# Every step of the two feed-forward layers given one part of the side work: conversion, activation and preparing of x

## The chip, the cores and the metric

One core of one Trainium2 chip runs the whole program. The metric is the device time of one execution in microseconds (us). TensorE (PE in the profile) multiplies; VectorE (DVE), ScalarE (ACT) and GpSimd (POOL) do the elementwise work; SyncE (SP) issues nearly all transfers. Each engine takes its instructions strictly in the order in which the program lists them, so an instruction that waits holds up all that stand behind it on its engine.

## The reference

Attention with a bucket mask (two batches, 8 heads, 768 positions, 64 wide) gives x of 1536 tokens by 512. Two feed-forward layers follow, each with 2048 hidden columns; their weights are given in double precision:

```
h = np.maximum(x @ w_in, 0.0)
x = (h * h @ w_out).astype(np.float32)
h = x @ w2_in
sp = np.where(h > 20.0, h, np.log1p(np.exp(np.minimum(h, 20.0))))
return ((h * np.tanh(sp)) @ w2_out).astype(np.float32)
```

## The kernel before

The attention fills the first 223 us or so and is untouched by the change. What follows works on each layer in 8 groups of 256 hidden columns, so groups 0 to 7 are the first layer and 8 to 15 the second. The tokens form three blocks of 512 (blk 0, 1 and 2).

Each matrix value is held as two float32r parts, a high and a low one, and each product is three matmuls (high by high, high by low, low by high).

**Steps.** The list `steps` sets the order of TensorE. A group has 26 steps of six matmuls: 7 `up` steps for blocks 0 and 1 together (128x512 tiles), 4 `down` steps for block 2 of the group before, 7 `up` steps for block 2 alone (128x256 tiles), then 8 `down` steps for blocks 0 and 1. Group 0 has no group before it and so 22 steps. In group 8 the 4 `down` steps stand ahead of the first `up` steps.

**Seven products for eight.** The product x @ w_in of a group is a 2 by 2 by 2 product of blocks, done in seven products (`SEVEN` says which sums of blocks go in, `USES` where each product is added). The seven sums of weight blocks are formed by `weigh` into the tile `wi`, the seven sums of x blocks by `prepare` into tiles `x`. Each `up` step writes a PSUM tile `m` (5 buffers). Its `use` runs behind the next step's matmuls: it copies `m` into `h` on ScalarE, adds it to `h` on VectorE, or adds one `h` to another (half of these on VectorE, half on GpSimd).

**Activation.** When an `h` is complete, `activate` has ScalarE compute the activation and the high part `gh`, and VectorE the low part `gl`. The `down` steps multiply `gh`, `gl` by the weight tile `wo` into a PSUM tile `acc` (3 buffers), which VectorE adds to `tot` (ScalarE copies it in the first group of a layer).

**Conversion.** Weights come as pieces of 128 by 512 doubles, four to a group (two for `w_in`, two for `w_out`), staged through two buffers `stg`. Each piece passes four parts: `begin` (absolute value on ScalarE into a tile `cv`, then a clamp to the range of the conversion on GpSimd; in the second layer GpSimd also adds, since ScalarE's table holds Mish there), `shift`, `low` and `end` on VectorE. `end` also issues the load of the piece after next, and for a `w_out` piece splits it into `wo` on GpSimd at once.

**Order.** Before the change a counter `due` grows by 23/26 with each step, and each whole unit of it takes the next entry of a queue (`conv_rest`: 8 parts, 7 `weigh`, 8 parts). `prepare` puts its sum, ScalarE's copy and VectorE's subtraction one behind the other into the same step. `activate` for one `h` at a time stands ahead of the matmuls' consumers of the next step.

Of the kernel before, what the change touches and what calls it, by code (L numbers as in the profile page):

```python
# [9 lines left out]
F32 = mybir.dt.float32  # L10
# [7 lines left out]
P = 128  # L18
# [5 lines left out]

EARLY = 4

XB = 2

CB = 5
GB = 5  # L30
# [30 lines left out]
def lsh_attention_relu2_mish_kernel(ctx, tc, qT, kT, vP, proj, w_in, w_out, w2_in, w2_out, out):  # L61
# [77 lines left out]

# [5 lines left out]
    def end(k):  # L145
        m, _, hi = work.pop(k)
        i, nm, c = pieces[k]
        mu = m.bitcast(U32)
        nc.vector.scalar_tensor_tensor(mu, hi, 0xC0000000, mu, ALU.bitwise_and, ALU.bitwise_or)  # L149
        stage(k + 2)  # L150
        if nm == "i":
            whole.setdefault(i, []).append(m)
            return
# [8 lines left out]
    def weigh(i, n):  # L162
# [4 lines left out]
        how = SEVEN[n][0]  # L167

        def block(b):
            return chain[i] if b == "chain" else whole[i][b[0]][:, b[1] * 256:(b[1] + 1) * 256]  # L170

        x = block(how[0])
        if len(how) > 1:
# [6 lines left out]
        nc.gpsimd.tensor_tensor(lo, x, b32(hi), ALU.subtract)  # L180


    conv = [
        [(nm, lambda part=part, k=4 * i + 2 * (nm == "o") + c: part(k)) for nm in "i" for c in range(FC) for part in parts]
        + [("i", lambda i=i, n=n: weigh(i, n)) for n in range(7)]
        + [("o", lambda part=part, k=4 * i + 2 + c: part(k)) for c in range(FC) for part in parts]
        for i in range(2 * NG)
    ]
    for i in range(EARLY // 4):
        conv[i] = []  # L190

    xf = [xy.tile([P, PPB, TB], F32, tag="xy", name=f"xf{i}") for i in range(NBLK)]

# [433 lines left out]
    for j in range(N):  # L627
# [23 lines left out]
        for when, n, k in conv_at:  # L651
            if when == j:
                if n < len(parts):
                    parts[n](k)
                else:
                    weigh(0, k)
        if bits is not None:
# [36 lines left out]
    def prepare(layer, unit, n, u):  # L694
# [14 lines left out]
        how = SEVEN[n][1]  # L709
        hi, lo, x = t[:, 0, u, :], t[:, 1, u, :], block(how[0])  # L710
        if len(how) > 1:
            if how[-1] == "chain":
                if "chain" not in (how[0], how[2]):
                    xchain[u] = xsum[0].tile([P, TB], F32, tag=f"chain{u}", name="chain", bufs=1)
                s = xchain[u]
            else:
                s = xsum[0].tile([P, TB], F32, tag="sum", name="sum")
            s = s[:, 0:w]
            (nc.vector if u else nc.gpsimd).tensor_tensor(s, x, block(how[2]), how[1])
            x = s  # L720
        nc.scalar.activation(hi, x, AF.Copy)
        nc.vector.tensor_tensor(lo, x, b32(hi), ALU.subtract)

    tot = {}
    xchain = {}
    xsum = []

    xs = {}
    prepare(0, 0, 0, 0)
    broadcast(*done, rp, N)  # L730
    prepare(0, 0, 0, 1)
    unstack(waiting, N - 1)
    for f in calls.pop(N):
        f()
    unstack(N // QT - 2, N)
    unstack(N // QT - 1, N)
    for u in range(2):
        prepare(0, 0, 1, u)
    for j in sorted(calls):
        for f in calls[j]:  # L740
            f()
# [24 lines left out]
    def up(i, unit, n):  # L766
# [8 lines left out]
        def use():  # L775
# [9 lines left out]
            ready.extend((i, blk, f) for f, blk in done.get(n, ()))  # L785

        return use

# [14 lines left out]
    def down(i, blk, c):  # L803
# [12 lines left out]
        def use():  # L816
# [44 lines left out]
    for i in range(2 * NG):  # L861
# [4 lines left out]
    at_step = {k: n for n, k in enumerate(steps)}  # L866
    behind, later, due = [], [], 0.0

    conv_rest = [(i, nm, f) for i, fs in enumerate(conv) for nm, f in fs]
    for n_step, (f, *a) in enumerate(steps):  # L870
        i = a[0]

        if f is up:
            while todo and (i // NG, a[1], a[2]) in [x[:3] for x in todo]:
                prepare(*todo.pop(0))
            while conv_rest and (conv_rest[0][0] < i or conv_rest[0][:2] == (i, "i")):
                conv_rest.pop(0)[2]()
        else:
            while (*a[:2], 0) in ready or (*a[:2], 1) in ready:
                later.append(activate(*ready.pop(0)))  # L880
            while later:
                later.pop(0)()
            while conv_rest and conv_rest[0][0] <= i:
                conv_rest.pop(0)[2]()

        pick = ready.pop(0) if ready and len(kept) < GB else None
        use = f(*a)
        if f is down and a[2] == PPB - 1:
            del kept[i, a[1], 0], kept[i, a[1], 1]
        while later:  # L890
            later.pop(0)()
        for g in behind:
            g()
        behind = [use]
        if pick is not None:
            if pick[0] == NG and loaded[-1] == EXP_SET:
                load_table(MISH_SET)
            later.append(activate(*pick))
        for _ in range(2):
            if todo:  # L900
                prepare(*todo.pop(0))
        due = min(due + 23 / 26, 4.0)
        while due >= 1 and conv_rest:
            k, nm, g = conv_rest[0]
            free = (up, k - 1, 0, 0) if nm == "i" else (down, k - 2, 2, PPB - 1)
            if at_step.get(free, -1) > n_step:
                break
            g()
            conv_rest.pop(0)
            due -= 1  # L910
    for g in behind + later:
        g()
    while ready:
        activate(*ready.pop(0))()
    last(2 * NG - 1, 2)

# ---- launch: one core; the host lays the inputs out and takes the output as it comes
# [41 lines left out]
```

## Time and profile before

| | |
|---|---|
| median of 3 runs | 991.13 us (990.05 to 991.76) |
| the profiled execution, its own time | 990.95 us |
| its span in the trace | 988.9 us |
| mean granted clock of TensorE | 0.887 of full speed |

The span leaves out 2.05 us of the time. The trace names groups by the tiles and lines; a step is six matmuls. The bracket behind a row of the timeline is the engine's idle time ahead of it and what ended that.

### The profile page before, as it was taken

The page shows a single profiled execution, that of the slowest core. Times are in us where ns is not written, and L with a number is a line of the kernel's source. Part 1 is how long each engine was busy: PE and PEld are TensorE (multiplying, and loading weights), DVE is VectorE, ACT ScalarE, POOL GpSimd, SP SyncE. Part 2 cuts the span into 40 slices and gives each one's busy share as a digit, 9 for nine tenths or more (in the row PEclk, how much of TensorE's full clock was granted, in tenths as well). Part 3 has the DMA queues.
Part 4 walks back from the last instruction along what each step waited for, and adds up shares of the span by engine and source line. Part 5 has one row for each costly group of instructions (what it writes and reads, how often), then busy time and mean ns, then how long its engine had stood idle before and what let it go on. Part 6 is the DMA issues. An engine that isn't in the chain of part 4 may idle for free.

```text
span 988.9 us, 11870 instructions
## 1 busy us (share of the span) xinstructions
PE 798.9 (81%) x3940; PEld 674.0 (68%) x3940; DVE 622.4 (63%) x1051; ACT 472.8 (48%) x879; POOL 584.9 (59%) x629
## 2 busy tenths in 40 slices
PE   9999999995697966969687686397868677686868
PEld 6999999992476755857566574376656566574757
DVE  8989989883735564654646576626464636364655
ACT  7988888892655343343434434444232323222221
POOL 9757885314364675656566564476666666666630
PEclk9999999996588989889798898598979797978889
DMA  7787687611011011111211111011011111111103
GB/s 214 170 217 196 163 203 179 161 37 29 21 43 65 23 63 43 43 64 43 65 43 43 50 39 36 26 43 64 23 63 43 43 43 43 43 43 42 43 1 127
DMA packets 29108, 72.76 MB, mean 74 GB/s; under 512 B 5064, under 2 KB 10536, under 8 KB 29048
## 3 DMA queue, kind: packets, MB, share of 16 engines
q1 hardware_dynamic: 28824, 71.88, 25.6%
q8 instruction: 31, 0.51, 0.2%
q14 instruction: 29, 0.24, 0.1%
q10 hardware_dynamic: 224, 0.13, 0.0%
HBM read 46.14 MB, written 3.19 MB: 50 GB/s over the span
## 4 chain that ended last, share of the span: by engine, by line
PE 38%; POOL 27%; DVE 20%; ACT 7%; issue 6%; DMA 1%; SPq 0%; DVEq 0%; POOLq 0%; ACTq 0%
PE acc L813 10%; POOL cv L131 7%; PE m L773 7%; PE s L427 6%; PE acc L482 6%; PE pT L453 6%; DVE h L783 4%; DVE gl L801 4%; POOL wo L158 3%; POOL wi L180 3%; POOL h L781 3%; DVE tot L824 3%; POOL sum L175 3%; POOL cv L129 3%; DVE cv L149 2%
## 5 line engine op out<-in xcount | busy, mean ns | idle before, releaser
L773 PE MATMUL m<-x,wi 128*128 128x512 f32 (+1 forms) x1344 | 288.5, 374 | 74.7 <-DVE h L783 47.1
L773 PEld LDWEIGHTS m<-x,wi 128*128 128x128 f32 x1344 | 237.8, 217 | 125.3 <-issue 47.4
L813 PE MATMUL acc<-gh,wo 128*128 128x512 f32 x384 | 134.6, 419 | 60.7 <-DVE tot L824 55.3
L813 PE MATMUL acc<-wo,gh 128*128 128x512 f32 x368 | 125.2, 424 | 48.8 <-DVE tot L824 47.0
L131 POOL TENSOR_SCALAR cv<-cv 128x512 f32<-128x512 f32 x63 | 123.3, 1957 | 30.2 <-ACT cv L123 25.8
L813 PEld LDWEIGHTS acc<-gh,wo 128*128 128x128 f32 x384 | 77.2, 201 | 84.1 <-DVE tot L824 59.3
L138 DVE TENSOR_SCALAR cv<-cv 128x512 uint32<-128x512 uint32 x64 | 33.8, 528 | 158.3 <-POOL cv L131 158.3
L783 DVE TENSOR_TENSOR h<-h,m 128x512 f32<-128x512 f32 (+1 forms) x160 | 86.6, 550 | 65.5 <-POOL h L781 52.9
L824 DVE TENSOR_TENSOR tot<-tot,acc 128x512 f32<-128x512 f32 x164 | 108.9, 681 | 22.2 <-PE acc L813 21.5
L813 PEld LDWEIGHTS acc<-wo,gh 128*128 128x128 f32 x368 | 75.2, 208 | 68.0 <-DVE tot L824 49.9
L801 DVE TENSOR_TENSOR gl<-h,gh 128x512 fp32r<-128x512 f32 x96 | 74.7, 778 | 49.3 <-ACT h L796 30.9
L470 DVE TENSOR_TENSOR pl<-pT,ph 128x768 fp32r<-128x768 f32 x96 | 91.7, 956 | 17.0 <-ACT ph L466 9.6
L779 ACT ACTIVATE h<-m 128x512 f32<-128x512 f32 (+1 forms) x128 | 55.5, 487 | 98.1 <-PE m L773 98.1
L157 POOL TENSOR_SCALAR wo<-cv 128x512 fp32r<-128x512 f32 x32 | 19.9, 623 | 135.4 <-DVE cv L149 129.4
L443 ACT ACTIVATE e<-e,nm 128x768 f32<-128x768 f32 x96 | 89.8, 935 | 7.9 <-DVE e L434 7.7
L798 ACT ACTIVATE h<-h 128x512 f32<-128x512 f32 x48 | 30.0, 625 | 132.1 <-DVE h L783 93.4
L434 DVE TENSOR_SCALAR_CACHE_REDUCE e<-s 128x768 f32<-128x768 f32 x96 | 90.9, 947 | 0.9 <-PE s L427 0.8
L781 POOL TENSOR_TENSOR h<-h 128x512 f32<-128x512 f32 (+1 forms) x32 | 32.2, 1007 | 98.6 <-DVE h L783 98.6
L466 ACT ACTIVATE ph<-pT 128x768 fp32r<-128x768 f32 x96 | 77.7, 809 | 12.7 <-PE pT L455 7.0
L813 PE MATMUL acc<-gl,wo 128*128 128x512 f32 x192 | 79.5, 414 | 0.0
L453 PE MATMUL pT<-ident,e 128*128 128x128 f32 x576 | 78.8, 273 | 0.3 <-DVE e L434 0.2
L813 PE MATMUL acc<-wo,gl 128*128 128x512 f32 x184 | 76.4, 415 | 0.0
(149 smaller groups left out, 1386.3 us busy)
## 6 DMA issues: line engine op xcount, KB each, us to landing
stg<-in_w_in_dram SPq DMA_DIRECT2D x32, 512.0 KB
stg<-in_w_out_dram SPq DMA_DIRECT2D x32, 512.0 KB
KA<-kh SPq DMA_DIRECT2D x28, 192.0 KB
v_r<-in_vP_dram SPq DMA_DIRECT2D x8, 384.0 KB
rb<-rd SPq DMA_DIRECT2D x32, 96.0 KB
out_dram<-tot SPq DMA_DIRECT2D x11, 256.0 KB
q_r<-in_qT_dram SPq DMA_DIRECT2D x7, 384.0 KB
k_r<-in_kT_dram SPq DMA_DIRECT2D x7, 384.0 KB
```

The lines of the kernel that those rows point to most:

```text
L131: nc.gpsimd.tensor_scalar(m, m, F64_LOW, F64_HIGH, ALU.max, ALU.min)
L434: nc.vector.tensor_scalar(e.rearrange("p (h s) -> p h s", s=H2), x, MASKED, None, ALU.min, ALU.min, accum_out=nm)
L443: nc.scalar.activation(e, e, AF.Exp, bias=nm, scale=-1.0, accum_out=ssums[p, half][:, c:c + 1])
L453: nc.tensor.transpose(ps[:, c * P:(c + 1) * P], e[:, c * P:(c + 1) * P], ident)
L466: nc.scalar.activation(ph, v, AF.Copy)
L470: nc.vector.tensor_tensor(pl, v, b32(ph), ALU.subtract)
L773: nc.tensor.matmul(m, WI[i][:, n, a, fs], x[:, b, u, :], start=u == k == 0, stop=u == 1 and k == 2)
L781: (nc.gpsimd if f else nc.vector).tensor_tensor(h, h, h_of(i, unit, *how), ALU.add)
L783: nc.vector.tensor_tensor(h, h, m, how)
L801: return lambda: nc.vector.tensor_tensor(gl, h, b32(gh), ALU.subtract)
L813: nc.tensor.matmul(acc, x, y, start=f == k == 0, stop=f == FC - 1 and k == 2)
L824: nc.vector.tensor_tensor(t, t, acc, ALU.add)
```

## The change

Every part of the side work gets a step of its own, from a fixed table of offsets (`conversion`), and GpSimd keeps only the splitting of weights, the sums of blocks that feed it, and the addition of the second layer's conversion.

- The clamp of the pieces converted in the feed-forward layers moves from GpSimd (`begin`) to VectorE (`shift`).
- The additions of one `h` to another all run on VectorE.
- `weigh_out` splits a `w_out` piece as an entry of its own, behind `end`.
- `prepare` is cut by two `yield`s into three steps: sum, copy, subtraction; the sums share one tag with 4 buffers.
- The low part `gl` is issued two steps after the activation (`halves`); an activation is taken one step after its `h` is complete, and only while fewer than 5 are live.

```
-XB = 2
+XB = 4
...
-        if k:
+        if 0 < k < EARLY:
             nc.gpsimd.tensor_scalar(m, m, F64_LOW, F64_HIGH, ALU.max, ALU.min)
...
-        if k == 0:
+        if not 0 < k < EARLY:
             nc.vector.tensor_scalar(m, m, F64_LOW, F64_HIGH, ALU.max, ALU.min)
...
+    def conversion(i):
+        k = 4 * i
+        at = [(o, f, (k + n,)) for n, os in enumerate(((0, 2, 3, 4), (2, 5, 6, 7), (6, 9, 10, 18), (19, 21, 22, 23)))
+              for o, f in zip(os, parts)]
+        at += [(o, weigh, (i, n)) for n, o in enumerate((8, 9, 10, 11, 12, 14, 16))]
+        return at + [(18, weigh_out, (i, 0)), (23, weigh_out, (i, 1))]
...
+            x = s[:, 0:w]
+        yield
         nc.scalar.activation(hi, x, AF.Copy)
+        yield
         nc.vector.tensor_tensor(lo, x, b32(hi), ALU.subtract)
...
-                    (nc.gpsimd if f else nc.vector).tensor_tensor(h, h, h_of(i, unit, *how), ALU.add)
+                    nc.vector.tensor_tensor(h, h, h_of(i, unit, *how), ALU.add)
...
+    for i in range(1, 2 * NG):
+        for o, g, a in conversion(i):
+            plan.setdefault((i - 1) * 26 + o, []).append(lambda g=g, a=a: g(*a))
...
+        halves.append((n + 2, k, activate(*k)))
+        live += 1
...
+        for g in behind:
+            g(n)
+        behind = [use]
+        for m, g in list(flow):
+            if next(g, g) is g:
+                flow.remove((m, g))
+        while halves and halves[0][0] <= n:
+            halves.pop(0)[2]()
+        for g in plan.pop(n, ()):
+            g()
+        if ready and ready[0][0] < n and live < GB:
+            take(n)
```

Since group 0 has 22 steps, an entry with offset o lands in step o + 4 of the group before the one that it converts for (an offset of 22 or 23 in step 0 or 1 of that group itself). TensorE's own order of matmuls is the same in both kernels.

VectorE at the border between two groups of the first layer, before. `tot` is the addition of a `down` step, L138, L143 and L149 are `shift`, `low` and `end`, L783 and L781 are the additions to `h`, L801 is `gl`:

```order
L801 TENSOR_TENSOR gl<-h,gh 128x512
L824 TENSOR_TENSOR tot_3587<-tot_3587,acc 128x512
L138 TENSOR_SCALAR cv<-cv 128x512
L824 TENSOR_TENSOR tot_3587<-tot_3587,acc 128x512
L143 SCALAR_TENSOR_TENSOR cv<-stg,cv 128x512
L824 TENSOR_TENSOR tot_3587<-tot_3587,acc 128x512
L149 SCALAR_TENSOR_TENSOR cv<-stg,cv 128x512
L824 TENSOR_TENSOR tot_3587<-tot_3587,acc 128x512
L138 TENSOR_SCALAR cv<-cv 128x512
L783 TENSOR_TENSOR h<-h,m 128x512
```

The same place of the changed kernel, where L830 is `tot`, L137 the clamp, L789 and L787 the additions to `h`, and L807 `gl`:

```order
L807 TENSOR_TENSOR gl<-h,gh 128x512
L137 TENSOR_SCALAR cv<-cv 128x512
L138 TENSOR_SCALAR cv<-cv 128x512
L830 TENSOR_TENSOR tot_3593<-tot_3593,acc 128x512
L143 SCALAR_TENSOR_TENSOR cv<-stg,cv 128x512
L149 SCALAR_TENSOR_TENSOR cv<-stg,cv 128x512
L789 TENSOR_TENSOR h<-h,m 128x512 x2
L787 TENSOR_TENSOR h<-h 128x512
L789 TENSOR_TENSOR h<-h,m 128x512
L787 TENSOR_TENSOR h<-h 128x512
L807 TENSOR_TENSOR gl<-h,gh 128x512
```

The clamp stands on VectorE right ahead of the shift, the second addition of `h` to `h` is there too, and a piece's parts no longer alternate with those of the next piece.

GpSimd around the same border, before: clamps (L131) between the splits of `wo` (L157, L158), the addition to `h` (L781), and the first split of `wi` (L179, L180):

```order
L131 TENSOR_SCALAR cv<-cv 128x512
L157 TENSOR_SCALAR wo_4559<-cv 128x512
L158 TENSOR_TENSOR wo_4559<-cv,wo_4559 128x512
L131 TENSOR_SCALAR cv<-cv 128x512
L157 TENSOR_SCALAR wo_4559<-cv 128x512
L158 TENSOR_TENSOR wo_4559<-cv,wo_4559 128x512
L781 TENSOR_TENSOR h<-h 128x512
L131 TENSOR_SCALAR cv<-cv 128x512 x2
L179 TENSOR_SCALAR wi_4744<-cv 128x256
```

GpSimd of the changed kernel at a border in the second layer, where L129 is the addition of `begin`, L159 and L160 the split of `wo`, and L177, L181, L182 the sums and splits of `wi`:

```order
L177 TENSOR_TENSOR sum<-cv,sum 128x256
L181 TENSOR_SCALAR wi_6085<-sum 128x256
L182 TENSOR_TENSOR wi_6085<-sum,wi_6085 128x256
L159 TENSOR_SCALAR wo_6209<-cv 128x512
L160 TENSOR_TENSOR wo_6209<-cv,wo_6209 128x512
L129 TENSOR_TENSOR cv<-cv,stg 128x512
L159 TENSOR_SCALAR wo_6209<-cv 128x512
L160 TENSOR_TENSOR wo_6209<-cv,wo_6209 128x512
L129 TENSOR_TENSOR cv<-cv,stg 128x512 x3
L181 TENSOR_SCALAR wi_6405<-cv 128x256
```

The clamps and the additions to `h` are gone; in the second layer the addition for the group's fourth piece stands behind all seven splits of `wi` and the first split of `wo`.

VectorE where the second layer's x is prepared, before (L722 is the subtraction of `prepare`, L719 its sum):

```order
L722 TENSOR_TENSOR x_5844<-chain,x_5844 128x512
L719 TENSOR_TENSOR chain<-tot_3587,tot_3540 128x512
L722 TENSOR_TENSOR x_5844<-chain,x_5844 128x512
L824 TENSOR_TENSOR tot_3725<-tot_3725,acc 128x512
L722 TENSOR_TENSOR x_5864<-chain,x_5864 128x512
L719 TENSOR_TENSOR chain<-tot_3587,chain 128x512
L722 TENSOR_TENSOR x_5864<-chain,x_5864 128x512
```

And in the changed kernel (L724 is the subtraction):

```order
L719 TENSOR_TENSOR sum<-tot_3593,tot_3550 128x512
L830 TENSOR_TENSOR tot_3729<-tot_3729,acc 128x512
L149 SCALAR_TENSOR_TENSOR cv<-stg,cv 128x512
L719 TENSOR_TENSOR sum<-tot_3593,sum 128x512
L830 TENSOR_TENSOR tot_3729<-tot_3729,acc 128x512
L724 TENSOR_TENSOR x_5853<-sum,x_5853 128x512 x2
L719 TENSOR_TENSOR sum<-tot_3593 128x512
L830 TENSOR_TENSOR tot_3729<-tot_3729,acc 128x512
```

Other work now stands between a sum and the subtraction that needs ScalarE's copy of it.

## Rows read from the trace of the kernel before

**Rows 1.** The page's first part: busy us, share of the span, instructions.

```profile
PE 798.9 (81%) x3940; PEld 674.0 (68%) x3940; DVE 622.4 (63%) x1051; ACT 472.8 (48%) x879; POOL 584.9 (59%) x629
```

**Rows 2.** Windows: stretch, length, busy us of each engine, clock, DMA share, GB/s.

```profile
223.48:290.69 67.21, 47.49 (x133) 30.46 (x133) 33.30 (x59) 31.71 (x63) 32.37 (x36) 0.64 0.09 26
458.32:501.45 43.13, 34.24 (x157) 28.31 (x156) 24.31 (x42) 16.87 (x30) 25.51 (x29) 0.88 0.16 49
590.29:656.90 66.61, 41.54 (x156) 33.15 (x157) 38.33 (x67) 28.64 (x56) 33.29 (x37) 0.74 0.10 32
680.26:685.30 5.04, 5.04 (x43) 5.03 (x42) 4.81 (x7) 2.86 (x8) 4.79 (x4) 1.00 0.16 47
794.52:842.18 47.66, 35.51 (x157) 29.55 (x156) 26.12 (x42) 13.17 (x24) 30.17 (x33) 0.86 0.14 45
937.66:988.90 51.24, 40.22 (x187) 33.34 (x185) 25.85 (x44) 10.84 (x20) 11.81 (x10) 0.93 0.17 62
```

**Rows 3.** Waits, 290 to 989 us: waiting line, releaser, total us, times, longest.

```profile
DVE cv L138 <- POOL cv L131: 158.3, 45, 6.3
...
PE acc L813 <- DVE tot L824: 102.3, 23, 8.2
...
DVE h L783 <- POOL h L781: 52.0, 29, 2.8
```

**Rows 4.** Timeline of one group, 462 to 484 us: start, length, instruction, idle before.

```profile
466.58 0.43 DVE L138 TENSOR_SCALAR cv<-cv 128x512 uint32<-128x512 uint32 x1 [3.58 <-POOL cv L131]
466.92 0.68 DVE L783 TENSOR_TENSOR h<-h,m 128x512 f32<-128x512 f32 x1
...
475.55 0.69 DVE L783 TENSOR_TENSOR h<-h,m 128x512 f32<-128x512 f32 x1 [2.71 <-POOL h L781]
477.55 0.43 DVE L138 TENSOR_SCALAR cv<-cv 128x512 uint32<-128x512 uint32 x1 [1.31 <-POOL cv L131]
...
480.29 0.68 DVE L824 TENSOR_TENSOR tot<-tot,acc 128x512 f32<-128x512 f32 x1
480.89 0.69 DVE L149 SCALAR_TENSOR_TENSOR cv<-stg,cv 128x512 uint32<-128x512 uint32 x1
...
481.03 0.79 PE L813 MATMUL acc<-gh,wo 128*128 128x512 f32 x1 [7.56 <-DVE tot L824]
```

**Rows 5.** TensorE's timeline, six steps at full clock and one behind a stall.

```profile
656.90 8.32 PE L773 MATMUL m<-x,wi 128*128 128x512 f32 x36
...
668.58 2.90 PE L773 MATMUL m<-x,wi 128*128 128x512 f32 x6 [3.35 <-DVE h L783]
```

**Rows 6.** Groups of instructions by form, 700 to 938 us: busy us, mean ns.

```profile
L131 POOL TENSOR_SCALAR cv<-cv 128x512 f32<-128x512 f32 x20 | 38.5, 1928 | 1.7
L129 POOL TENSOR_TENSOR cv<-cv,stg 128x512 f32<-128x512 f32 x21 | 27.0, 1287 | 0.0
...
L158 POOL TENSOR_TENSOR wo<-cv,wo 128x512 fp32r<-128x512 f32 x10 | 12.9, 1290 | 0.8
...
L783 DVE TENSOR_TENSOR h<-h,m 128x256 f32<-128x256 f32 x25 | 10.1, 420 | 10.9 <-PE m L773 5.8 <-POOL h L781 4.6
```

**Rows 7.** The one clamp that ran on VectorE, in the attention: min/median/max ns.

```profile
L137 DVE TENSOR_SCALAR cv<-cv x1: 416/416/416, 25.8 to 25.8; 128x512 f32<-128x512 f32 x1
```

**Rows 8.** Timeline, GpSimd and VectorE side by side at two places.

```profile
479.99 2.16 POOL L131 TENSOR_SCALAR cv<-cv 128x512 f32<-128x512 f32 x1 [2.48 <-ACT cv L123]
...
769.72 1.28 POOL L129 TENSOR_TENSOR cv<-cv,stg 128x512 f32<-128x512 f32 x1
769.79 1.49 DVE L138 TENSOR_SCALAR cv<-cv 128x512 uint32<-128x512 uint32 x1 [2.56 <-POOL cv L131]
```

**Rows 9.** A load of `stg`: its issue, and the last slice with its traffic.

```profile
462.46 0.33 SPq L112 DMA_DIRECT2D stg<-in_w_in_dram  x1
...
465.00:466.00 1.00, 1.00 (x6) 0.83 (x5) 0.00 (x0) 0.00 (x0) 1.00 (x1) 1.00 0.19 74
```

**Rows 10.** Timeline: the first sum of x blocks in group 0.

```profile
233.36 1.26 POOL L719 TENSOR_TENSOR chain<-xf,xf 128x512 f32<-128x512 f32 x1
```

More of the change, by code (lines that the diff above doesn't have):

```diff
@@ L150, in end, with weigh_out @@
         stage(k + 2)
-        if nm == "i":
-            whole.setdefault(i, []).append(m)
-            return
+        whole.setdefault((i, nm), []).append(m)
+    def weigh_out(i, c):
+        m = whole[i, "o"][c]
         if c == 0:
@@ L169, in block @@
         def block(b):
-            return chain[i] if b == "chain" else whole[i][b[0]][:, b[1] * 256:(b[1] + 1) * 256]
+            return chain[i] if b == "chain" else whole[i, "i"][b[0]][:, b[1] * 256:(b[1] + 1) * 256]
         x = block(how[0])
@@ L654, in lsh_attention_relu2_mish_kernel @@
                     parts[n](k)
+                    if (n, pieces[k][1]) == (len(parts) - 1, "o"):
+                        weigh_out(0, pieces[k][2])
                 else:
@@ L711, in prepare, with prepare_now @@
         if len(how) > 1:
+            y = block(how[2])
+            s = xchain[u] if how[0] == "chain" else xsum[0].tile([P, TB], F32, tag="sum", name="sum")
             if how[-1] == "chain":
[L713 to L720, printed above, removed]
+                xchain[u] = s
+            (nc.vector if u else nc.gpsimd).tensor_tensor(s[:, 0:w], x, y, how[1])
+            x = s[:, 0:w]
+        yield
         nc.scalar.activation(hi, x, AF.Copy)
+        yield
         nc.vector.tensor_tensor(lo, x, b32(hi), ALU.subtract)
+    def prepare_now(*a):
+        for _ in prepare(*a):
+            pass
     tot = {}
@@ L728, in lsh_attention_relu2_mish_kernel @@
     xs = {}
-    prepare(0, 0, 0, 0)
+    prepare_now(0, 0, 0, 0)
     broadcast(*done, rp, N)
-    prepare(0, 0, 0, 1)
+    prepare_now(0, 0, 0, 1)
     unstack(waiting, N - 1)
@@ L737, in lsh_attention_relu2_mish_kernel @@
     for u in range(2):
-        prepare(0, 0, 1, u)
+        prepare_now(0, 0, 1, u)
     for j in sorted(calls):
@@ L773, in up, with use @@
                 nc.tensor.matmul(m, WI[i][:, n, a, fs], x[:, b, u, :], start=u == k == 0, stop=u == 1 and k == 2)
-        def use():
+        def use(now):
             for (f, j), how in USES[n]:
@@ L784, in use @@
             done = {1: ((0, 0),), 4: ((1, 1),), 5: ((1, 0),), 6: ((0, 1),)} if not unit else {5: ((1, 2),), 6: ((0, 2),)}
-            ready.extend((i, blk, f) for f, blk in done.get(n, ()))
+            ready.extend((now, (i, blk, f)) for f, blk in done.get(n, ()))
         return use
@@ L814, in down, with use @@
         layer, g = divmod(i, NG)
-        def use():
+        def use(now):
             if g == 0 and c == 0:
@@ L865, in lsh_attention_relu2_mish_kernel @@
         steps += [(down, i, blk, c) for blk in range(2) for c in range(PPB)]
[L866 to L870, printed above, removed]
+    plan, behind, flow, live = {}, [], [], 0
+    for i in range(1, 2 * NG):
+        for o, g, a in conversion(i):
+            plan.setdefault((i - 1) * 26 + o, []).append(lambda g=g, a=a: g(*a))
+    halves = []
@@ L871, in lsh_attention_relu2_mish_kernel, with release, take @@
+    def release():
+        nonlocal live
+        live -= FC
+    def take(n):
+        nonlocal live
+        k = ready.pop(0)[1]
+        if k[0] == NG and loaded[-1] == EXP_SET:
+            load_table(MISH_SET)
+        halves.append((n + 2, k, activate(*k)))
+        live += 1
+    for n, (f, *a) in enumerate(steps):
         i = a[0]
         if f is up:
[L874 to L877, printed above, removed]
-        else:
[L879 to L884, printed above, removed]
@@ L886, in lsh_attention_relu2_mish_kernel @@
-        pick = ready.pop(0) if ready and len(kept) < GB else None
+            want = (i // NG, a[1], a[2])
+            while any(x[:3] == want for x in todo):
+                while flow:
+                    for _ in flow.pop(0)[1]:
+                        pass
+                flow.append((todo[0], prepare(*todo.pop(0))))
+                next(flow[-1][1])
+            while any(x[:3] == want for x, _ in flow):
+                for _ in flow.pop(0)[1]:
+                    pass
+        else:
+            while any(k[:2] == (i, a[1]) for _, k in ready):
+                take(n)
+            while any(k[:2] == (i, a[1]) for _, k, _ in halves):
+                halves.pop(0)[2]()
@@ L887, in lsh_attention_relu2_mish_kernel @@
         use = f(*a)
[L888 to L891, printed above, removed]
         for g in behind:
-            g()
[L894 to L898, printed above, removed]
+            g(n)
[3 more added lines that the diff above has]
+                flow.remove((m, g))
@@ L899, in lsh_attention_relu2_mish_kernel @@
+        while halves and halves[0][0] <= n:
+            halves.pop(0)[2]()
+        for g in plan.pop(n, ()):
+            g()
+        if ready and ready[0][0] < n and live < GB:
+            take(n)
         for _ in range(2):
             if todo:
[L901 to L910, printed above, removed]
@@ L911, in lsh_attention_relu2_mish_kernel @@
-    for g in behind + later:
-        g()
+                flow.append((todo[0], prepare(*todo.pop(0))))
+                next(flow[-1][1])
+        if f is down and a[2] == PPB - 1:
+            plan.setdefault(n + 2, []).append(release)
+    for g in behind:
+        g(len(steps))
     while ready:
-        activate(*ready.pop(0))()
+        take(len(steps))
+    while halves:
+        halves.pop(0)[2]()
     last(2 * NG - 1, 2)
```

8 lines of the change are left out of this document (removed).

## The prediction

> **What bounds the kernel now.** I read the page's busy shares first: TensorE is at 81%, no other engine above 63% [rows 1]. So no engine is full; something makes them take turns. The windows by group say where: a group of the first layer takes 43.13 us with 34.24 of TensorE, one of the second 47.66 with 35.51, and the granted clock is below full in both, 0.88 and 0.86 [rows 2]. At full clock six steps of 512 columns take 8.32 us less the 0.16 by which the last runs past its successor's start, so 1.36 a step; the seven half-width steps take 5.04 at clock 1.00 [rows 2, 5]. A group is 19 x 1.36 + 5.04 = 30.9 us of pure TensorE. Of 43 to 48 us, 12 to 17 are stalls and the half clock behind them: after a gap of 3.35 us one step took 2.90 [rows 5].
>
> The waits name the cause. VectorE waited 158.3 us for GpSimd's clamp (L131) and 52.0 for GpSimd's addition to `h`; TensorE waited 102.3 us for VectorE's `tot`, 8.2 at a time [rows 3]. The timeline of one group shows it as one chain: VectorE stands at L138 or L783 until GpSimd is done, the `tot` that frees an `acc` buffer is queued behind it at 480.29, and TensorE starts at 481.03 after 7.56 idle [rows 4]. VectorE was not busy, it was held. A stall that comes once per group, with its clock loss, is what the change can remove.
>
> **What the change costs, by engine and group.** VectorE starts one 128x512 instruction with two inputs every 0.60 us (480.29 to 480.89), and a one-input one takes 0.34 to the next start (466.58 to 466.92) [rows 4]; a 128x256 one, 0.42 long [rows 6], I take at 0.34 too, with the same overlap of 0.08. The clamp on VectorE: the only row is 0.416 long [rows 7], against 1.928 on GpSimd [rows 6]. That bounds it from 0.34 (packed) to 1.93 (as on GpSimd); it has the form of L138 on the same engine, so I take 0.34. VectorE after: 33 wide instructions x 0.60 (12 `tot`, 5 + 2 on `h`, 6 `gl`, 8 of `low` and `end`), 7 half-width x 0.34, 8 of clamp and shift x 0.34: 19.8 + 2.4 + 2.7 = 24.9 us packed, against 24.31 busy now [rows 2]. It still fits under 30.9.
>
> GpSimd loses 4 x 1.93 and two additions, about 1.29 by the like-sized L158 [rows 6] and half of that: 25.51 - 7.7 - 1.9 = 15.9 us in the first layer, 30.17 - 9.6 = 20.6 in the second [rows 2]. ScalarE is unchanged at 13 to 17 us. No DMA is added. TensorE becomes the longest at 30.9.
>
> I then walked one group through, step by step, with these durations. In the first layer every VectorE instruction has its input when its turn comes, except short waits of under 1 us; VectorE falls 3 to 4 us behind around the half-width steps, which are only 0.72 us each, and is level again by the next group. The 5 `m` and 3 `acc` buffers cover about that much. GpSimd's splits of `wi` start behind `end` of the first piece and are done some 4 us ahead of the next group. The one new thing is that VectorE and GpSimd now work at the same time. Where they did so before, L138 took 1.49 instead of 0.43 while GpSimd's L129 ran, 1.06 more [rows 8]. Elsewhere L149 kept 0.69 beside a clamp under way [rows 4, 8]. With 26 VectorE instructions in a group that read two SBUF tensors, or one in the fast form, and GpSimd busy half the time with instructions of 0.4 to 1.3 us, I put 1 us on TensorE for this: **32 us a group in the first layer**; bounds 30.9 (none) and 36 (rival 1).
>
> In the second layer a loop comes close. `end` of a group's first piece issues the load of its third, only two steps ahead of its `begin`. Issue to last traffic is about 3.1 us [rows 9]; then 0.7 on ScalarE, 1.29 for L129, then on GpSimd in order all seven splits (20.6 less 4 x 1.29 and two `wo` splits of 1.29 + 0.6: 11.7), one `wo` split 1.9, L129 of the fourth piece 1.3; VectorE, which stands at that shift, then needs 2.5 for clamp, shift, `tot`, `low`, `end`, and 12 wide instructions and a clamp with shift (7.9) to the next `end` of a first piece. Sum 30.4 with no contention at all, against 30.9; with 2 to 4 us of mutual hold-ups the loop is the longer: **34 us a group in the second layer**, bounds 30.9 and 38.
>
> Group 0: from the first sum at 233.36 [rows 10] VectorE has 33 wide, 25 half-width and 3 clamp-and-shift pairs: 30.4 us, so it sets the end of the `up` steps at 263.8; 8 `down` steps add 10.9, slow clock and waits 2 to 3: ends at 277 instead of 290.69, so 54 us from 223.5 instead of 67.2 [rows 2]. Here the split of `prepare` matters: sum, copy and subtraction no longer stand in lockstep.
>
> Group 8, where x of the second layer is prepared: 66.6 us now [rows 2]. In its first 18 steps TensorE needs 11 x 1.36 + 5.04 = 20.0, VectorE 32 x 0.60 + 25 x 0.34 + 3 x 0.68 = 29.8; ten behind, of which the rest of the group absorbs some, plus a clock loss: 43.
>
> Group 15 converts nothing for a successor; with the last tile and the output it takes 51.24 now, 40.22 of it TensorE's [rows 2]. I take 41.
>
> **Sum.** Before: 223.5 + 67.2 + 299.6 (groups 1 to 7, to 590.29) + 66.6 + 280.8 (9 to 14, to 937.66) + 51.2 = 988.9. After: 223.5 + 54 + 7 x 32 + 43 + 6 x 34 + 41 = 789.5 us of span. The profiled execution has 2.05 us outside its span; its 990.95 is 0.2 below the median. Forecast **792 us**, 20% less; own range 770 to 820.
>
> **The rule that speaks against it.** The Trainium skill (SBUF — State Buffer, section "Who interferes with whom") says that a VectorE instruction in a two-port mode, or with two SBUF inputs, and a GpSimd instruction that reads SBUF exclude each other for the whole length of the one that starts first. By that rule 16 x 0.60 + 10 x 0.34 = 13.0 us of VectorE and 15.9 or 20.6 of GpSimd in a group could not overlap at all; the result is rival 1's. The 1.06 us on L138 agrees with it, L149 beside the clamp does not.
>
> **Rivals.**
> 1. *VectorE becomes the bound through contention.* If each of those 26 instructions waits for half a GpSimd instruction (0.4 us) whenever GpSimd is busy (half to two thirds of the time), 5.2 to 7 us come to 24.9: 30 to 32 us with no slack, so each unevenness is a TensorE stall with half clock behind it, 36 to 38 us a group. That is 4.5 more for 13 groups: 792 + 58 = 850 us. For it: the 1.49 row. Against: such a row is rare before. Chance 0.18 (830 to 900).
> 2. *Everything hides.* 31 us in all groups, 38 in group 8: 792 - 7 - 18 - 5 = 762. For it: TensorE ran the attention and long stretches without a gap. Against: the loop of the second layer. Chance 0.15 (750 to 770).
> 3. *The lockstep only moves.* The parts have their own steps, but a fixed table cannot wait, and VectorE stands at L137 for ScalarE or GpSimd as it stood at L138 for the clamp. If half of the 12 to 17 us stay, 38 to 40 us a group and 900 us in all. The walk found no such wait in the first layer. Chance 0.04.
> 4. *Slower.* The load of the third piece, issued two steps ahead, lands late; ScalarE waits at its `begin` with the activation and the `h` copies behind it, and through the loop every group lengthens. Slower than before needs a loop of 48 us in the second layer and 44 in the first, so a landing time of about 17 us instead of 3.1. The DMA share is at most 0.17 in this stage [rows 2], so nothing speaks for it. Chance 0.02. No change within 0.2%: 0.01.
>
> **Chances and range.** Forecast 0.60, rivals as given. The range reaches down to rival 2 and up to rival 1's centre: 756 to 850, which leaves out about 0.05 below and 0.13 above. A measurement tells 0.2% (2 us) from no change: faster 0.97, same 0.01, slower 0.02.
>
> **What would show it.** In the changed profile: TensorE's stalls of 7 to 8 us in the group's last `down` steps of block 2 gone, and its granted clock near 1.00 in the first layer; VectorE's largest waits on TensorE, no longer on GpSimd; clamps of about 0.42 us; first-layer groups of 31 to 33 us, second-layer ones 1 to 3 longer, with VectorE waiting at the shift of a fourth piece for L129. VectorE's instructions lengthened by more than 0.2 us on average would show rival 1. A second layer as short as the first would refute the loop. The prediction is wrong if group length stays above 36 us, or if group 0 or 8 gains nothing, since then the lockstep of `prepare` was not their limit.

## The result: 839.96 us, and the profile after

The changed kernel takes 839.96 us (median of 4 runs, 839.68 to 840.98), the kernel before 990.76 beside it: a ratio of 0.848, 95% interval 0.846 to 0.849. It is 15% faster; the forecast was 20% (792 us). The time lies 48 us above that point: inside the whole range (756 to 850), but outside the forecast's own 770 to 820, and where rival 1 was put (830 to 900).

The page's first line, which answers to [rows 1]:

```profile
PE 756.3 (90%) x3940; PEld 646.8 (77%) x3940; DVE 704.8 (84%) x1143; ACT 469.3 (56%) x879; POOL 458.3 (55%) x536
```

GpSimd's work fell by 127 us, and VectorE's rose by 82, to 84% of a shorter span. The windows answer to [rows 2]: group 0, group 3, group 5, group 8, group 11 and group 15 with the last tile (columns as there: stretch, length, busy us of TensorE, its weight loads, VectorE, ScalarE, GpSimd, clock, DMA share, GB/s):

```profile
223.93:286.70 62.77, 41.04 (x133) 30.07 (x133) 43.52 (x67) 32.08 (x64) 30.23 (x33) 0.67 0.12 36
353.44:388.57 35.13, 32.98 (x158) 27.57 (x156) 29.41 (x49) 16.54 (x30) 16.74 (x22) 0.95 0.18 60
422.19:455.83 33.64, 31.26 (x158) 26.37 (x157) 29.34 (x49) 16.57 (x30) 16.75 (x22) 1.00 0.18 63
524.61:583.09 58.48, 41.57 (x157) 31.78 (x156) 52.02 (x80) 27.82 (x56) 30.49 (x32) 0.82 0.11 37
653.77:689.14 35.37, 31.73 (x157) 26.33 (x156) 30.39 (x49) 13.10 (x24) 22.29 (x27) 1.00 0.18 60
797.70:837.90 40.20, 36.57 (x187) 31.22 (x185) 25.64 (x43) 10.64 (x20) 4.73 (x4) 0.99 0.21 79
```

A group of the first layer went from 43.13 to 33.64 us, with TensorE's clock at 1.00 instead of 0.88; one of the second from 47.66 to 35.37. Not all are like that: groups 3 and 6 take 35.1 us at a clock of 0.95, and groups 12 and 13 of the second layer stand at 0.95 too, with 37.0 and 36.6 us. The ends of the windows give the forecast's terms one by one (group 8 begins with the first `down` step of block 2 at 524.61; the expectations below that give it 60.6 us count it from 522.50):

| stretch | forecast us | measured us | off by |
|---|---|---|---|
| group 0 | 54 | 62.8 | +8.8 |
| groups 1 to 7 (286.70 to 524.61) | 224 | 237.9 | +13.9 |
| group 8 | 43 | 58.5 | +15.5 |
| groups 9 to 14 (583.09 to 797.70) | 204 | 214.6 | +10.6 |
| group 15 and the last tile | 41 | 40.2 | -0.8 |

The waits from 286 to 838 us answer to [rows 3]:

```profile
PE acc L819 <- DVE tot L830: 30.1, 18, 2.4
...
DVE h L789 <- PE m L779: 21.2, 13, 2.0
DVE tot L830 <- PE acc L819: 19.0, 34, 0.9
DVE cv L137 <- POOL cv L129: 15.8, 12, 2.5
```

TensorE waits 30.1 us for VectorE's `tot` instead of 102.3, and 2.4 at most instead of 8.2. VectorE's 158.3 us at the clamp and 52.0 at GpSimd's additions are gone; what is left of GpSimd is L129, 15.8. The timeline of group 5 around its one stall (start, length, instruction; in brackets the idle time before) shows what stands there now:

```profile
441.24 0.85 DVE L137 TENSOR_SCALAR cv<-cv 128x512 f32<-128x512 f32 x1
...
442.43 0.79 POOL L182 TENSOR_TENSOR wi<-sum,wi 128x256 fp32r<-128x256 f32 x1
442.55 1.22 DVE L807 TENSOR_TENSOR gl<-h,gh 128x512 fp32r<-128x512 f32 x1
...
443.30 1.07 POOL L177 TENSOR_TENSOR sum<-sum,cv 128x256 f32<-128x256 f32 x1
...
443.69 1.22 DVE L143 SCALAR_TENSOR_TENSOR cv<-stg,cv 128x512 uint32<-128x512 uint32 x1
...
448.11 1.27 DVE L830 TENSOR_TENSOR tot<-tot,acc 128x512 f32<-128x512 f32 x2
...
448.84 0.50 PE L819 MATMUL acc<-gh,wo 128*128 128x512 f32 x1 [2.38 <-DVE tot L830]
```

VectorE is never idle here. A clamp takes 0.85 us instead of 0.42, a `gl` and a `low` 1.22 instead of 0.69, each beside a GpSimd instruction. VectorE runs late, the first `tot` of block 0 comes at 448.11, and TensorE, with its three `acc` buffers full, stands for 2.38 us. Two things can be behind that lateness: the lengthening, or simply that too much of VectorE's work stands in these steps. The experiments separate them.

### The profile page after: what moved, and what is told of

Its sections match the earlier page's. It is cut to its first block, busy times and chain, and to the rows that moved or that the text cites. A ratio compares the mean times of both kernels' runs of the same rounds, so it can differ in the third digit from the quotient of the medians.

```text
span 837.9 us, 11917 instructions
## 1 busy us (share of the span) xinstructions
PE 756.3 (90%) x3940; PEld 646.8 (77%) x3940; DVE 704.8 (84%) x1143; ACT 469.3 (56%) x879; POOL 458.3 (55%) x536
## 4 chain that ended last, share of the span: by engine, by line
PE 50%; DVE 33%; issue 6%; DMA 6%; ACT 3%; POOL 1%; DVEq 0%; SPq 0%; POOLq 0%; ACTq 0%
PE acc L819 16%; PE m L779 10%; PE acc L482 7%; PE s L427 7%; DVE h L789 7%; PE pT L453 7%; DVE h L787 5%; DMA stg<-in_w_out_dram 4%; DVE cv L143 4%; DVE x L724 4%; DVE gl L807 3%; DVE tot L830 3%; DVE cv L137 2%; DVE cv L149 2%; DVE sum L719 1%
## 5 line engine op out<-in xcount | busy, mean ns | idle before, releaser
L779 PE MATMUL m<-x,wi 128*128 128x512 f32 (+1 forms) x1344 | 263.1, 353 | 38.5 <-DVE x L724 16.9
L779 PEld LDWEIGHTS m<-x,wi 128*128 128x128 f32 x1344 | 220.7, 199 | 79.3 <-DVE x L724 25.2
L819 PE MATMUL acc<-gh,wo 128*128 128x512 f32 x384 | 126.5, 402 | 14.1 <-DVE tot L830 14.1
L819 PE MATMUL acc<-wo,gh 128*128 128x512 f32 x368 | 118.7, 405 | 18.7 <-DVE tot L830 16.0
L830 DVE TENSOR_TENSOR tot<-tot,acc 128x512 f32<-128x512 f32 x164 | 109.7, 680 | 19.3 <-PE acc L819 19.0
L789 DVE TENSOR_TENSOR h<-h,m 128x512 f32<-128x512 f32 (+1 forms) x160 | 86.2, 549 | 31.6 <-PE m L779 21.8
L819 PEld LDWEIGHTS acc<-gh,wo 128*128 128x128 f32 x384 | 74.5, 194 | 32.9 <-DVE tot L830 17.3
L819 PEld LDWEIGHTS acc<-wo,gh 128*128 128x128 f32 x368 | 70.2, 195 | 37.7 <-DVE tot L830 20.7
L807 DVE TENSOR_TENSOR gl<-h,gh 128x512 fp32r<-128x512 f32 x96 | 81.6, 850 | 20.7 <-ACT h L802 14.1
L819 PE MATMUL acc<-gl,wo 128*128 128x512 f32 x192 | 76.9, 400 | 3.3 <-DVE gl L807 3.3
L129 POOL TENSOR_TENSOR cv<-cv,stg 128x512 f32<-128x512 f32 x29 | 41.0, 1417 | 65.4 <-ACT cv L128 55.8
L819 PE MATMUL acc<-wo,gl 128*128 128x512 f32 x184 | 73.7, 400 | 0.0
L453 PEld LDWEIGHTS pT<-ident,e 128*128 128x128 f32 x576 | 67.5, 140 | 6.0 <-DVE e L434 1.6
L159 POOL TENSOR_SCALAR wo<-cv 128x512 fp32r<-128x512 f32 x32 | 20.2, 631 | 83.1 <-DVE cv L149 83.1
L181 POOL TENSOR_SCALAR wi<-cv 128x256 fp32r<-128x256 f32 x48 | 23.8, 496 | 64.8 <-DVE cv L149 63.2
```

The source lines that it names most:

```text
L453: nc.tensor.transpose(ps[:, c * P:(c + 1) * P], e[:, c * P:(c + 1) * P], ident)
L807: return lambda: nc.vector.tensor_tensor(gl, h, b32(gh), ALU.subtract)
L830: nc.vector.tensor_tensor(t, t, acc, ALU.add)
```

## Experiments

Lines of a kernel with a longer table or added lines stand 6 or 7 lower in its trace (L819 is L825 or L826).

### What each part of the change is worth

**The clamp back on GpSimd**, everything else as changed:

```diff
-        if 0 < k < EARLY:
+        if k:
             nc.gpsimd.tensor_scalar(m, m, F64_LOW, F64_HIGH, ALU.max, ALU.min)
...
-        if not 0 < k < EARLY:
+        if k == 0:
             nc.vector.tensor_scalar(m, m, F64_LOW, F64_HIGH, ALU.max, ALU.min)
```

> Changed kernel with the clamp of every piece back on GpSimd (1.93 us each there, four a group, before the shift), and all else as changed: order by steps, prepare in three parts, h+h on VectorE. If the clamp's move is the bigger part of the gain of 150 us (GpSimd's 7.7 us a group on the way to VectorE's shift), it comes out above 925 us, with VectorE's shift waiting for GpSimd in each group again. If the order by steps carries most of it, GpSimd's clamps lie in steps where nobody waits for them and it comes out between 840 and 885 us.

883.5 us; ratio to the kernel before 0.892 (0.890 to 0.893). The waits from 290 us on:

```profile
DVE cv L138 <- POOL cv L131: 72.2, 33, 5.2
```

That is the upper end of what was expected if the order carries most of it. VectorE stands at the shift as in [rows 3], for 72 us instead of 158. So the rest of the change takes half of that wait away by itself; the clamp's move takes the other half, and 43.5 us of time. What the table of steps, the later `gl` and the limit on live activations give each was not run apart.

**The old order with the clamp on VectorE**: the kernel before, with the change's two conditions on the clamp, in `begin` and `shift`, and nothing else of it:

> Kernel before, with one edit alone: the clamp of the pieces on VectorE (0.42 us instead of 1.93 on GpSimd). Its h+h additions for the second half of the features stay on GpSimd and its order stays the one written by due times. If the clamp is the bigger part: under 900 us. If the order carries most of it: 930 to 990 us, with VectorE still waiting for GpSimd's splits and additions, and TensorE's stalls of 7 us shortened but there.

917.4 us, 0.926 (0.924 to 0.927), between the two expectations. The waits from 290 us on:

```profile
PE acc L813 <- DVE tot L824: 81.3, 23, 7.7
...
DVE cv L137 <- POOL cv L129: 51.6, 20, 4.4
DVE h L783 <- POOL h L781: 50.4, 27, 2.8
```

The clamp alone gives 74 us, and stalls of up to 7.7 us remain, behind the additions to `h` and L129. The rest of the change alone (the run before) gives 108. Together they give 151, not 181: both shorten the same waits.

**The second half's h+h additions back on GpSimd:**

```diff
-                    nc.vector.tensor_tensor(h, h, h_of(i, unit, *how), ALU.add)
+                    (nc.gpsimd if f else nc.vector).tensor_tensor(h, h, h_of(i, unit, *how), ALU.add)
```

> Changed kernel with the h+h additions for the second half of the features back on GpSimd (two of 512 or 256 columns in each set of seven products), all else as changed. They queue behind the splits of the weights, which now have fixed steps: if that queue matters, VectorE's next addition to the same h waits some 1 to 3 us twice or more a group, and it comes out at 870 to 930 us. If VectorE's load is what sets the 33.6 us of a group, taking two to four instructions of 0.69 us a group off it makes the kernel faster than 840 us, by up to 15 groups x 1.4 us: 820.

865.3 us, 0.874 (0.870 to 0.877): 25 us slower than the changed kernel, a little less than expected. VectorE has less to do and is late all the same:

```profile
DVE h L789 <- POOL h L787: 44.5, 29, 3.4
```

**Preparing x in one step again** (`prepare_now(*todo.pop(0))` where the changed kernel appends to `flow`):

> Changed kernel with preparing of x in one step again (sum, copy and remainder issued together), all else as changed. This bears on groups 0 and 8 alone (62.8 and 60.6 us). If spreading preparing over steps is what lets these groups flow, they get 8 to 15 us longer each: 856 to 870 us. If VectorE's and GpSimd's load in these groups sets their length, the order of the three parts hardly matters: 836 to 846 us.

856.3 us, 0.864 (0.862 to 0.866). Group 0 takes 68.8 instead of 62.8 us, less than the 8 us more that were expected, and groups 7 and 8 together 102.3 instead of 92.1. Sixteen us of the gain are in `flow`.

### Where the missing 48 us went

**No splits beside VectorE.** For groups 3 to 15 the weights' splits and the sums that feed them are left out, and those of two groups before are used again:

```diff
     def weigh_out(i, c):
+        if i > 2:
+            WO[i] = WO[i - 2]
+            return
...
     def weigh(i, n):
+        if i > 2:
+            WI[i] = WI[i - 2]
+            return
```

> Changed kernel without GpSimd's splits of the weights from the fourth group of either layer's row on (the split weights of two groups before are used again, so these groups' products are not the reference's); VectorE's instructions, the loads and the order are all there. Theory (GpSimd's work beside VectorE lengthens VectorE's instructions, its backlog fills the three accumulators, and TensorE stalls some 2 us a group): groups 3 to 7 go from 33.6 to 31.0 to 31.5 us, groups 9 to 14 from 35.6 to 32 or 33, and it comes out at 795 to 812 us. Rival (VectorE's load is simply bunched in these steps, contention or not): groups stay above 33 and 34.5 us, 825 to 840 us.

805.1 us, 0.812 (0.810 to 0.814). Windows of a group of either layer:

```profile
448.53:480.89 32.36, 31.47 (x158) 26.41 (x157) 26.53 (x49) 16.55 (x30) 0.00 (x0) 1.00 0.21 65
630.74:663.95 33.21, 31.75 (x158) 26.34 (x157) 27.96 (x49) 12.87 (x24) 5.69 (x4) 1.00 0.19 64
```

The same 49 VectorE instructions take 26.53 us instead of 29.34. By form, from 320 to 520 us (busy us, mean ns), in the changed kernel:

```profile
L830 DVE TENSOR_TENSOR tot<-tot,acc 128x512 f32<-128x512 f32 x68 | 45.5, 679 | 6.2 <-PE acc L819 6.1
L807 DVE TENSOR_TENSOR gl<-h,gh 128x512 fp32r<-128x512 f32 x35 | 27.4, 782 | 4.1 <-ACT h L802 3.8
...
L143 DVE SCALAR_TENSOR_TENSOR cv<-stg,cv 128x512 uint32<-128x512 uint32 x24 | 19.6, 817 | 0.0
L137 DVE TENSOR_SCALAR cv<-cv 128x512 f32<-128x512 f32 x24 | 15.8, 659 | 0.0
```

and without splits:

```profile
L836 DVE TENSOR_TENSOR tot<-tot,acc 128x512 f32<-128x512 f32 x74 | 49.5, 682 | 5.1 <-PE acc L825 5.1
L813 DVE TENSOR_TENSOR gl<-h,gh 128x512 fp32r<-128x512 f32 x36 | 24.7, 687 | 8.4 <-ACT h L808 8.4
...
L143 DVE SCALAR_TENSOR_TENSOR cv<-stg,cv 128x512 uint32<-128x512 uint32 x25 | 17.1, 685 | 0.0
...
L137 DVE TENSOR_SCALAR cv<-cv 128x512 f32<-128x512 f32 x25 | 10.5, 420 | 0.0
```

What reads two SBUF tensors, and the clamp, are longer beside GpSimd; `tot`, whose one input is in PSUM, is 0.68 either way. This is the clearest part of the shortfall, and the time came in the middle of what the theory gave. Groups 1 to 7 get 11.4 us shorter together. In the changed kernel neither VectorE nor TensorE waits for GpSimd there, so this is the lengthening. But groups 3 to 6 stop at 32.2 us on average, above the 31.0 to 31.5 expected and 1.2 above TensorE's own 31: not all of it is contention. In the second layer, where groups 9 to 14 get 15.4 us shorter, the run does not part two causes, since L129 no longer stands behind splits either: VectorE's waits for it fall from 13.3 to 3.8 us.

**One accumulator more, one `m` buffer fewer** (`pacc` 4 and `psh` 4 instead of 3 and 5):

> Changed kernel with four accumulators for the down products and four for the up products (three and five before), all else as changed. If the stall of 2.1 to 2.4 us a group at the fourth product of block 0 is there because a backlog of VectorE finds just three accumulators, one more takes 1 to 2 us of it away in each of 14 groups: 812 to 830 us. If VectorE needs the time anyway, or four buffers for the up products make a new wait of the same length there: 836 to 846 us.

830.6 us, 0.838 (0.836 to 0.840), just past the upper end of what the backlog gave. In the first layer the stall at `acc` is gone and groups 1 to 6 take 32.8 us instead of 34.0; stalls of 0.7 to 0.8 at `m` stand in its place, twice a group.

**Late loads.** First the third piece's begin two steps later, the first piece's end a step earlier and two of VectorE's parts a step later, then the begin alone:

```diff
-((0, 2, 3, 4), (2, 5, 6, 7), (6, 9, 10, 18), (19, 21, 22, 23))
+((0, 2, 3, 3), (2, 5, 6, 7), (8, 10, 11, 18), (19, 21, 22, 23))
...
+((0, 2, 3, 4), (2, 5, 6, 7), (8, 9, 10, 18), (19, 21, 22, 23))
```

> Changed kernel with the third piece's begin two steps later (steps 8, 10, 11, 18 for 6, 9, 10, 18) and the first piece's end one step earlier (step 3 for 4), so that its load has five steps (about 6.4 us) instead of two to land. If ScalarE's wait for this load (3 to 6 us in most groups: 62 us in all from 270 us on) holds its copies of h and through them TensorE: groups get 1 to 2 us shorter, 815 to 830 us. If VectorE's hold-ups set the group's length: 836 to 843 us, with ScalarE's waits for loads gone.

> Changed kernel with one number of the table changed: the third piece's begin at step 8 instead of 6, so that its load has four steps instead of two. VectorE's instructions stand at the same places as in the changed kernel. If the load that lands late is what cost first-layer groups 2 us (ScalarE stands at its copy of the piece, and the copies of h behind it come late): groups 3 to 6 go from 34.4 to 32.8 us as with the later third piece, 826 to 832 us. If it was VectorE's two parts one step later that gave those 10 us: 836 to 843 us, with groups of 33.6 to 35 us as before.

The first gives 829.2 us, 0.837 (0.835 to 0.839), the second 842.8, 0.850 (0.849 to 0.852), no better than the changed kernel. ScalarE's wait for the load, 290 to 520 us, in the changed kernel and in the second:

```profile
ACT cv L123 <- DMA stg<-in_w_out_dram: 27.2, 6, 5.2
```

```profile
ACT cv L123 <- DMA stg<-in_w_out_dram: 6.5, 7, 1.4
```

The wait goes, and no time with it. The load was late and off the path; the first kernel's 11 us come from what it has beyond that, two of VectorE's parts a step further on, and one a step earlier, with the load that it issues. These were not tried apart.

**VectorE's parts where a step is long.** The full-width steps take 1.36 us, the seven half-width ones 0.72, and the table put many parts into these. For the conversion of groups 3 to 15:

```diff
+        (((-10, -8, -7, -6), (-7, -5, -4, -3), (-3, -1, -1, 2), (7, 9, 10, 14)), (-2, -1, 0, 1, 3, 4, 6), (7, 15)),
```

(the steps of the four pieces' parts, of the splits of `wi` and of those of `wo`; a negative step lies in the group before; a row for group 2, which leads over, is left out here).

> Changed kernel with another table of steps for groups 3 on: VectorE's parts of the conversion go from the dense steps (up products of half width, TensorE 0.65 us a step) to the eight down steps at a group's end and the first steps of the next, where a step is 1.28 us and VectorE has one addition; the splits follow six steps earlier. If where VectorE's work lies decides (a backlog in the dense steps spills into the accumulators): groups 3 to 7 at 31.5 to 32.5 us, groups 9 to 14 at 33 to 34.5, 812 to 828 us. If contention costs VectorE the same wherever the splits lie: 834 to 845 us.

830.7 us, 0.838 (0.837 to 0.840), between the two expectations: the first layer did better than either, the second worse. Windows of groups 5 and 11, and `gl` by form from 320 to 520 us:

```profile
418.62:449.64 31.02, 31.02 (x157) 26.27 (x156) 30.09 (x50) 16.81 (x30) 17.93 (x23) 1.00 0.22 69
642.04:678.30 36.26, 33.00 (x158) 27.73 (x156) 31.23 (x50) 13.12 (x24) 23.36 (x26) 0.95 0.19 59
```

```profile
L813 DVE TENSOR_TENSOR gl<-h,gh 128x512 fp32r<-128x512 f32 x37 | 38.0, 1027 | 1.2 <-ACT h L808 1.2
```

In the first layer TensorE does not stop once: 31.02 us busy of 31.02, while VectorE's instructions are longer than ever (`gl` 1.03 us instead of 0.78). So contention costs TensorE nothing where VectorE's work is spread; it costs where a full stretch has no room for it. The second layer did not gain (36.3 us a group instead of 35.8): over groups 9 to 14 VectorE stands at the shifts for L129 for 16.2 us instead of 13.3, and TensorE waits for `tot` for 20.8 instead of 16.0. Group 1, where the table goes over, takes 38.3 us.

**All sums of x on VectorE**, for groups 0 and 8 (`nc.vector.tensor_tensor(s[:, 0:w], x, y, how[1])` for both halves), then the same without the splits for groups 3 to 15, as above:

> Changed kernel with all sums of preparing x on VectorE (the ten of the one half are on GpSimd in the changed kernel). This bears on groups 0 and 8 (62.8 and 60.6 us). In group 8 a GpSimd sum of 1.67 to 1.74 us runs beside VectorE instructions that take 1.6 to 2.4 us instead of 0.6. If mutual hold-ups make group 8 long, five sums of 0.60 and five of 0.34 us more on VectorE cost less than they free: groups 0 and 8 get 1 to 5 us shorter each, 830 to 838 us. If VectorE's plain load sets these groups, they get up to 4.7 us longer each: 842 to 849 us.

> Changed kernel with all sums of preparing x on VectorE and, from the fourth group of products on, without GpSimd's splits of the weights (those of two groups before are used again, so the products are not the reference's). In group 8 GpSimd then runs beside VectorE in two instructions alone. Theory: of group 8's 60.6 us some 13 are VectorE instructions lengthened by GpSimd (VectorE's instructions from 522.5 to 576.9 us sum to 39.8 at 0.60 and 0.34 us each, and it stood idle for 1.0): group 8 comes to 46 to 50 us, and it comes out at 792 to 802 us. Rival (VectorE waits in these groups for ScalarE's copies and for TensorE, and GpSimd has little to do with it): group 8 stays at 52 to 58 us, 803 to 812 us.

The first: 839.0 us, 0.846 (0.842 to 0.849), no difference that can be told. In its profiled execution (841.3 us) group 0 is 2.7 us shorter, groups 7 and 8 together as long as before, and groups 9 to 14 are 3.9 us longer. The second: 804.1 us, 0.811 (0.810 to 0.813); groups 7 and 8 together take 84.1 us, with the splits left out alone 83.8, in the changed kernel 92.1. In group 8 of the changed kernel GpSimd and VectorE stood side by side like this:

```profile
539.01 1.67 POOL L719 TENSOR_TENSOR sum<-sum,tot 128x512 f32<-128x512 f32 x1 [0.63 <-DVE x L724]
...
539.57 1.67 DVE L719 TENSOR_TENSOR sum<-sum,tot 128x512 f32<-128x512 f32 x1
```

Both take 1.67 us instead of 1.26 [rows 10] and 0.69. With GpSimd all but silent, VectorE's stretch up to the last addition to `h` fell from 51.9 us (522.69 to 574.62) to 43.8 (508.50 to 552.29), although four wide and four half-width sums, 3.8 us, had come to it. But group 8 did not reach the 46 to 50 us expected: it takes 52.0, and 51.6 with the splits left out alone. Both the group and the time, 804.1, lie where the rival was put. Of group 8's 58.5 us some 7 went with the splits, and none that can be told with GpSimd's sums.

**A second form of the table**, gentler at the start, and with the shift of the third and fourth piece five steps behind its begin (the row for groups 4 to 15, against the last row of the first form; the rows for groups 2 and 3 are left out here):

```diff
-(-3, -1, -1, 2), (7, 9, 10, 14)), (-2, -1, 0, 1, 3, 4, 6), (7, 15)
+(-3, 2, 2, 8), (9, 14, 15, 16)), (-2, -1, 0, 1, 3, 4, 6), (9, 17)
```

> The table with VectorE's parts in the down steps, in a second form: the second and third group's tables go over to it in smaller steps, and the shift of the third and of the fourth piece stands five steps behind its begin instead of two, so that in the second layer VectorE no longer stands there for GpSimd's addition (two waits of 1.3 us a group with the first form). Expected: first-layer groups of 31.0 to 31.5 us from the fourth on, group 1 at 33 to 34 instead of 38.2, groups 9 to 14 at 33.0 to 34.5 instead of 36.4, groups 0 and 8 as they were: 808 to 818 us. If the waits for GpSimd only move to other places in the second layer, its groups stay above 35.5 us: 822 to 832 us.

822.99 us (5 runs), 0.830 (0.829 to 0.831): faster than both kernels, and slower than the 808 to 818 expected.

```profile
419.68:451.58 31.90, 31.52 (x157) 26.20 (x156) 30.04 (x49) 16.73 (x30) 18.19 (x22) 1.00 0.21 67
642.10:676.43 34.33, 32.15 (x157) 26.05 (x156) 31.29 (x49) 12.53 (x24) 22.70 (x27) 1.00 0.19 62
```

VectorE no longer waits for L129, and the second layer takes 34.5 us a group on average, instead of 35.8 in the changed kernel and 36.3 with the first form; the first layer gives back 0.9 us of what the first form gained. Which of the moved parts costs that was not tried.

## Why the prediction held, and where its sizes were off

**The mechanism was right.** VectorE was held, not busy; with the clamp and the additions off GpSimd and the parts in steps of their own, the stalls of 7 to 8 us went, and with them most of the half clock (four of the 13 groups still have a clock of 0.95). The runs of the parts show that no single one does it. The size was not right: the forecast proper, 770 to 820 us with a chance of 0.60, missed, and the whole range held the time because it was drawn up to the middle of rival 1's.

**Pure TensorE 30.9 us a group:** measured 31.02, where a table leaves no stall.

**"I put 1 us on TensorE" for contention (groups 1 to 7, +13.9).** VectorE grows by 2.8 us a group, and a group takes 34.0 on average, 3.0 above TensorE's own 31. The step that failed lies in the walk: it found VectorE 3 to 4 us behind around the half-width steps and said that the buffers "cover about that much", and then put the contention on top as if it fell anywhere. It falls in these very steps, with the splits, and takes the backlog past the three `acc` buffers. One buffer more takes 1.1 us a group of it away, VectorE's parts elsewhere (groups 3 to 7) all of it.

**34 us in the second layer (+10.6).** The loop through L129 is there: VectorE waits at the shift for it. But it waits 13.3 us over groups 9 to 14, about 2 a group, and its removal in the last table gave 1.3 (along with other moves). Without splits a group takes 33.2, 2.6 less, but that run shortens the loop as well as the contention. VectorE's work is 2.4 us shorter in it (30.39 to 27.96 in group 11), its waits at L129 1.6 a group. Which of the two is the larger term stays open.

**Group 0 (+8.8) and group 8 (+15.5).** Here I priced nothing for contention. Group 8 had a miscount too: "in its first 18 steps" VectorE has not 32 but 43 wide instructions (14 of L724, 4 sums, 6 `tot`, 5 `gl`, 7 of `low` and `end`, 7 on `h`), 25 half-width ones and 4 pairs of clamp and shift, 37.0 us at 0.60, 0.34 and 0.68 instead of 29.8. It took 51.9, 14.9 more; with GpSimd nearly silent, 40.8 us of work took 43.8, so some 12 of the 14.9 are GpSimd's, and 3 would be there without it. VectorE began 1.9 us ahead of TensorE's start on the group, and its last addition left 8.5 us to the group's end, where the forecast left 13: 37.0 + 14.9 - 1.9 + 8.5 = 58.5. In group 0 the `up` steps ended at 274.14 instead of 263.8; that 1.9 to 2.7 us went with the sums on VectorE is all that was tried there, so its split between contention and ScalarE's and VectorE's turns stays open.

**The rivals.** Rival 1 named the cause of the shortfall with a larger price: its 36 to 38 us a group came from 5.2 to 7 us of hold-ups and half clock behind each stall, there were 2.8, and in most groups no half clock. The time came out in its band all the same, because groups 0 and 8 were too low in the forecast that it was added to. The Trainium skill's rule (SBUF — State Buffer, section "Who interferes with whom") has the right instructions: two SBUF inputs, or a two-port mode, and, on the other side, none for an instruction with at most one SBUF input outside these modes; by that rule the trace agrees (`gl`, `low` and the clamp longer, `tot` 0.679 against 0.682). That the two exclude each other is borne out as well: in the rows around group 5's stall each ends 0.5 to 0.6 us behind the other (the `gl` at 443.77 behind the split's end at 443.22, GpSimd's sum at 444.37 behind the `gl`, `low` at 444.91 behind that sum), as if they took turns. The sum stays at 2.8 us a group because most of VectorE's instructions of these kinds meet none of GpSimd's. The clamp on GpSimd is the exception, as the prediction saw: the last section has its rows. Rival 4's late load was real (ScalarE waited up to 5.2 us for it) and cost nothing. Rivals 2 and 3 fell.

**What I said would show it.** Right: clamps (median 0.428 us), the clock in most groups, VectorE's waits, second-layer groups 1 to 3 us longer. Wrong: first-layer groups of 31 to 33, they took 34.0. The mean lengthening over 49 instructions is 0.06 us, far under the 0.2 set for rival 1, and yet 35 us went when the splits went: a mean over the group was the wrong thing to ask for.

## What to carry to other kernels

When two engines stop waiting for each other, they start to run beside each other; price that in the steps where both have most to do, not as a mean over the group. Where a table fixes the order, count each engine's work per step against the step's length: a stretch that is full already has no room for a hold-up, and the same hold-up costs nothing where there is slack. A wait that shows in the list (here for a load) is worth a run that takes it away by itself, before anything is built on it.

## What the runs showed of the hardware

Contention is mutual: GpSimd's 128x512 sum went from 1.26 to 1.67 us beside VectorE's, and VectorE's from 0.69 to 1.67.

GpSimd's clamp held VectorE far less. In the run with the clamp back on GpSimd, two clamps of 1.92 us stood beside a `gl` and a `low` with two SBUF inputs, which kept their 0.68 (an addition to `h` and a shift between them took 0.86 and 0.50 instead of 0.69 and 0.43):

```profile
331.93 3.80 POOL L131 TENSOR_SCALAR cv<-cv 128x512 f32<-128x512 f32 x2 [1.15 <-ACT cv L123]
...
333.01 0.68 DVE L807 TENSOR_TENSOR gl<-h,gh 128x512 fp32r<-128x512 f32 x1
...
335.22 0.68 DVE L143 SCALAR_TENSOR_TENSOR cv<-stg,cv 128x512 uint32<-128x512 uint32 x1
```

TensorE's clock behind a stall was not settled by the stall's length. Group 5's 2.38 us left the window's clock at 1.00, and so did 3.29 us ahead of 528.29 in group 8 (524.77 to 535.00). Group 3's 2.13 us were followed by 3.15 us (380.10 to 383.25) at 0.50, half of full speed, as the 3.35 us of [rows 5] were:

```profile
380.10 0.80 PE L819 MATMUL acc<-gh,wo 128*128 128x512 f32 x1 [2.13 <-DVE tot L830]
```
